# A planned instruction order is planned again: another cost table, a pause ahead of one kind of product, and a closing pair that takes its products in turn

## The chip, the cores and the metric

The kernel runs on one core of one Trainium2 chip. The metric is device time in microseconds (us) of the whole program; less is better. Times before the change are the median of three runs; the profile is of one more execution.

## The reference

Random-feature attention for 4 batches, 8 heads, 576 tokens, head size 64 and 128 features, then two layers of a two-matrix network over the 2304 tokens (width 512, inner width 2048):

```python
def phi(x):
    proj = np.einsum('bhsd,md->bhsm', x, omega)
    h = proj - np.sum(x * x, axis=-1, keepdims=True) / 2.0
    return np.exp(h - np.max(h, axis=-1, keepdims=True)) / np.sqrt(m)
q_p, k_p = (phi(q_s), phi(k_s))
kv = np.einsum('bhsm,bhsd->bhmd', k_p, v); z = np.sum(k_p, axis=2)
num = np.einsum('bhsm,bhmd->bhsd', q_p, kv)
den = np.einsum('bhsm,bhm->bhs', q_p, z)[..., None] + 1e-06
x = (num / den)            # to (2304, 512)
x = leaky_relu(x @ w1_in) @ w1_out
h = x @ w2_in
out = (h * np.clip(h + 3.0, 0.0, 6.0) / 6.0) @ w2_out
```

## The kernel before, in words

The tokens are cut into five row groups (GN: 512, 256, 512, 512, 512). Attention of a group makes its rows; **layer one** (moe1) runs group by group, with the attention of the next group put between its matmuls; **layer two** (moe2) follows in the order 0, 2, 3, 4, 1, so that the last row group is the one with 256 rows. Every large product is three matmuls (high by high, low by high, high by low part of fp32 numbers split in two).

In layer two a 512-row group takes its products by a scheme with seven products for a 2x2 block product. `Hpair` makes two blocks of the inner width: seven products of six matmuls each of 256 columns (line 1122), into three half banks R[0], R[1], R[2]. R[0] is used for four products in turn. Each is added onto the sum that the bank holds, and between them `save` copies R[0] out with ScalarE (`late_u<-bank`). So the second product into R[0] has to wait until the first one's copy is done, the third for the second one's, the fourth for the third one's. `parts` splits the result into two tiles of the kind g, with four additions of 128 columns (line 472 where GpSimd does them). `down` makes the seven products of the second matrix, three matmuls each (line 1044), and `finish` adds them up and stores them (lines 1065, 1069). The last row group has `Hsingle` (plain products, lines 478 to 480, 256 columns) instead of `Hpair`.

Nothing of the order is written by hand. Each step is an `op` with a due time, the engines that may do it and a cost on each; `Graph.run` keeps a clock for every engine and takes the step that can start first. All instructions are issued in that order, and each engine does its own in order. On TensorE, attention steps inside layer one are held back by SLACK, and by FOLLOW right behind another attention step, so that they come in groups; SWITCH is the planner's price for a change between attention and layers. `keep_warm` (line 1317) puts in matmuls on a zero tile where the planner sees TensorE idle before layer one begins: 15 at the start, and later one for every 326 ns of a gap. BIAS is what a step must save before it goes to VectorE; T0, L1, ATT, SG, UP, DOWN, XLEAD, SOON and READY are the due times; CAP and `room` set how many buffers a kind has.

## Time and profile before

| what | value |
|---|---|
| median of 3 runs | 907.85 us (905.75 to 908.74) |
| profiled execution, device time | 907.79 us |
| its span, first to last instruction | 906.0 us |
| TensorE busy | 892.0 us of the span |
| VectorE, ScalarE, GpSimd busy | 617.0, 492.8, 332.0 us |

The span is what the trace shows; 1.8 us of the device time lie around it. Matmuls are pipelined: one of 256 columns is shown some 280 ns long while the next one starts 113 to 118 ns after it. So a stretch is read by the starts of the instructions and by how many there are in it, not by the busy share, which is near 100% at any pace.

### The profile page before, as it was taken

The page shows a single profiled execution, that of the slowest core. Times are in us where ns is not written, and L with a number is a line of the kernel's source. Part 1 is how long each engine was busy: PE and PEld are TensorE (multiplying, and loading weights), DVE is VectorE, ACT ScalarE, POOL GpSimd, SP SyncE. Part 2 cuts the span into 40 slices and gives each one's busy share as a digit, 9 for nine tenths or more (in the row PEclk, how much of TensorE's full clock was granted, in tenths as well). Part 3 has the DMA queues.
Part 4 walks back from the last instruction along what each step waited for, and adds up shares of the span by engine and source line. Part 5 has one row for each costly group of instructions (what it writes and reads, how often), then busy time and mean ns, then how long its engine had stood idle before and what let it go on. Part 6 is the DMA issues. An engine that isn't in the chain of part 4 may idle for free.

```text
span 906.0 us, 17804 instructions
## 1 busy us (share of the span) xinstructions
PE 892.0 (98%) x6349; PEld 796.2 (88%) x6349; DVE 617.0 (68%) x1464; ACT 492.8 (54%) x1155; POOL 332.0 (37%) x559
## 2 busy tenths in 40 slices
PE   8999999999999999999999999999999999999998
PEld 8878888889777877888888888999999999999997
DVE  5998877877897976555687344675665658666554
ACT  6966674866776555544455345543443444445442
POOL 3454454544535321101010003244426436454642
PEclk9999999999999999999999999999999999999999
DMA  9556644677557555978899349885786684677540
GB/s 333 152 167 215 204 153 139 208 228 232 149 171 223 178 166 178 367 286 314 292 343 349 95 140 326 280 296 168 244 311 218 201 260 131 224 242 231 167 134 28
DMA packets 91497, 198.01 MB, mean 219 GB/s; under 512 B 14736, under 2 KB 40976, under 8 KB 91408
## 3 DMA queue, kind: packets, MB, share of 16 engines
q1 hardware_dynamic: 91408, 196.87, 65.7%
q8 instruction: 50, 0.82, 0.4%
q14 instruction: 39, 0.32, 0.1%
HBM read 150.18 MB, written 46.66 MB: 217 GB/s over the span
## 4 chain that ended last, share of the span: by engine, by line
PE 91%; DVE 4%; ACT 2%; issue 1%; DMA 1%; POOL 1%; SPq 0%; DVEq 0%; POOLq 0%; ACTq 0%
PE bank L1044 18%; PE bank L1122 17%; PE bank L478 15%; PE bank L480 15%; PE bank L479 15%; PE bank L721 4%; PE bank L768 1%; PE bank L949 1%; PE bank L918 1%; PE bank L790 1%; DVE junk L892 1%; PE bank L844 1%; DMA late_w<-in 1%; DVE nm L686 1%; PE bank L779 0%
## 5 line engine op out<-in xcount | busy, mean ns | idle before, releaser
L1044 PE MATMUL bank<-w,g 128*128 128x256 f32 x762 | 108.1, 279 | 0.4 <-DVE g L467 0.2
L1044 PEld LDWEIGHTS bank<-w,g 128*128 128x128 f32 x762 | 96.9, 188 | 1.0 <-DVE g L467 0.7
L464 ACT COPY late_u<-bank 128x256 f32<-128x256 f32 (+1 forms) x112 | 43.1, 386 | 95.1 <-PE bank L1122 86.4
L986 DVE TENSOR_TENSOR g<-bank,g 128x512 fp32r<-128x512 f32 (+1 forms) x80 | 50.8, 635 | 60.9 <-ACT g L464 60.2
L984 ACT ACTIVATE bank<-bank 128x512 f32<-128x512 f32 (+1 forms) x80 | 43.8, 548 | 76.2 <-PE bank L480 76.0
L1122 PE MATMUL bank<-x,late_w 128*128 128x256 f32 x552 | 74.0, 281 | 0.9 <-DVE u L1065 0.7
L697 ACT ACTIVATE h<-bank,nm 128x128 f32<-128x128 f32 x228 | 63.5, 390 | 18.9 <-POOL nm L692 18.7
L1122 PEld LDWEIGHTS bank<-x,late_w 128*128 128x128 f32 x552 | 68.2, 189 | 1.5 <-DVE u L1065 0.9
L1122 PE MATMUL bank<-second_w,late_w 128*128 128x256 f32 x498 | 68.5, 281 | 0.5 <-ACT late_u L464 0.5
L478 PE MATMUL bank<-g,w 128*128 128x512 f32 (+1 forms) x180 | 68.9, 383 | 0.0
L478 PE MATMUL bank<-x,w 128*128 128x512 f32 (+1 forms) x180 | 68.7, 382 | 0.1
L480 PE MATMUL bank<-g,w 128*128 128x512 f32 (+1 forms) x180 | 66.3, 368 | 0.8 <-DVE g L986 0.8
L480 PE MATMUL bank<-x,w 128*128 128x512 f32 (+1 forms) x180 | 66.4, 369 | 0.5 <-POOL x L468 0.5
L479 PE MATMUL bank<-g,w 128*128 128x512 f32 (+1 forms) x180 | 66.2, 368 | 0.0
L479 PE MATMUL bank<-x,w 128*128 128x512 f32 (+1 forms) x180 | 66.2, 368 | 0.0
L1122 PEld LDWEIGHTS bank<-second_w,late_w 128*128 128x128 f32 x498 | 62.4, 189 | 0.8 <-ACT late_u L464 0.7
L686 DVE TENSOR_REDUCE nm<-bank 128x4 f32<-128x512 f32 (+2 forms) x76 | 48.1, 654 | 15.8 <-PE bank L721 15.7
L1044 PE MATMUL bank<-second_w,g 128*128 128x256 f32 x333 | 48.8, 280 | 0.0
L903 POOL TENSOR_TENSOR h<-h,den 128x512 f32<-128x512 f32 (+2 forms) x32 | 33.1, 1038 | 41.8 <-DVE den L898 25.4
L692 POOL TENSOR_TENSOR nm<-nm,sq 128x4 f32<-128x4 f32 (+2 forms) x76 | 25.2, 344 | 60.2 <-DVE nm L689 57.2
L478 PE MATMUL bank<-x,second_w 128*128 128x512 f32 (+1 forms) x120 | 45.2, 377 | 0.3 <-ACT h L697 0.3
L472 POOL TENSOR_TENSOR xr<-late_xr 128x128 f32<-128x128 f32 x38 | 19.3, 526 | 70.7 <-DVE late_xr L1160 70.7
(361 smaller groups left out, 2449.9 us busy)
## 6 DMA issues: line engine op xcount, KB each, us to landing
late_w<-in SPq DMA_DIRECT2D x84, 512.0 KB, 4.5
in<-late_w SPq DMA_DIRECT2D x32, 512.0 KB, 3.8
late_w<-in SPq DMA_DIRECT2D x40, 256.0 KB, 4.5
third_w<-in SPq DMA_DIRECT2D x20, 512.0 KB, 4.4
wst<-w2i SPq DMA_DIRECT2D x16, 512.0 KB, 4.2
wst<-w2o SPq DMA_DIRECT2D x16, 512.0 KB, 4.1
x_t<-late_w SPq DMA_DIRECT2D x12, 512.0 KB, 4.5
wst<-w1i SPq DMA_DIRECT2D x10, 512.0 KB, 4.6
```

The source lines that it names most:

```text
L464: return [("act", c_act(n, psum), lambda: nc.scalar.copy(dst(), src())), dve if psum else dve + (True,)]
L478: nc.tensor.matmul(o, lhsT=ah, rhs=bh, start=start, stop=False)
L479: nc.tensor.matmul(o, lhsT=al, rhs=bh, start=False, stop=False)
L480: nc.tensor.matmul(o, lhsT=ah, rhs=bl, start=False, stop=stop)
L686: g.op([("dve", c_dve(c * 128), lambda raw=raw, n_=n_: nc.vector.tensor_reduce(out=n_()[:, :, 0], in_=raw(), axis=AX.X, op=ALU.min))], rd= ...
L697: nc.scalar.activation(h.tiles[0][:, q * 128:q * 128 + 128], raw()[:, q], AF.Exp, bias=nm.tiles[0][:, q], scale=-1.0)
L721: nc.tensor.matmul(ps[bank].tiles[0][o, at:at + 128], lhsT=src.tiles[0][r, k * one + i * 128:k * one + i * 128 + n], rhs=wn[r], start=True ...
L903: eng.tensor_tensor(out=x, in0=x, in1=den.tiles[1][:, 0:c].to_broadcast([128, c, 128]), op=ALU.mult)
L984: g.op([("act", c_act(n, True), lambda: nc.scalar.activation(P(), P(), AF.Prelu, alpha=0.01))], wr=[p], due=d)
L986: g.op([("dve", c_dve(n), lambda: nc.vector.tensor_tensor(out=G1(), in0=P(), in1=G0().bitcast(F32), op=ALU.subtract))], rd=[p, (gg, 0)], w ...
L1044: nc.tensor.matmul(acc[bank].tiles[0][:, half * 256:half * 256 + 256], lhsT=src.tiles[x][:, q * 128:q * 128 + 128], rhs=w[k].tiles[y][:, c ...
L1122: nc.tensor.matmul(R[r](), lhsT=w[x], rhs=m[y], start=start and k == n == 0, stop=k == 1 and n == 2, skip_group_check=True)
```

## The change

The planner gets another table of numbers and four new rules. (1) TensorE steps of attention have a mode: S (scores, 64-row tiles), N (the products with 64-column tiles) or F (the others); a table TURN gives the price of each change of mode, and WAIT, MATE and FOLLOW say how long a step waits for company. (2) `Hpair` gives every later product into R[0] a lag of APART, 100 ns of the planner's time, so that other work goes between. (3) In the last row group the last two pairs take products 4 to 7 in turn, with due times 100 ns apart, in the order b11, t2, t3, b21, t1, t4, b22. (4) `finish` of that group has a tile more for its sums and another order of additions. Besides, the transposed inputs of the first stage have four buffers for three, LAT is 165 for 150, BIAS2 200 for 300, and due times and buffer counts differ. The arithmetic is the same.

```diff
-SLACK = 2000.0
-FOLLOW, SWITCH = 400.0, 110.0
+SLACK = 1.0
+PACE = 2.215
+WAIT = {"S": 4000.0, "N": 1000.0, "F": 1500.0}
+FOLLOW = 400.0
+MATE = 400.0
+TURN = {("M", "S"): 193.0, ("M", "N"): 92.0, ("S", "M"): 205.0, ("N", "M"): 158.0, ("F", "S"): 193.0, ("F", "N"): 97.0, ("S", "F"): 175.0,
...
-NW1 = 10
+NW1 = 11
-BIAS2 = 300.0
+BIAS2 = 200.0
-UP, DOWN = 7.2e3, 2.5e3
+UP, DOWN = 7100.0, 2600.0
+APART = 100.0
-LAG_A, XLEAD, SOON, READY = 3.0, 9e3, 10e3, 14e3
+LAG_A, XLEAD, SOON, READY = 2.5, 6000.0, 13000.0, 15000.0
...
-    LAT = 150.0
+    LAT = 165.0
-    CAP = {"x2": 5, "s": 2, "h": 4, "sum": 4, "raw": 6}
+    CAP = {"x2": 6, "s": 1, "h": 6, "sum": 4, "raw": 6}
...
-                at = o.ready + (FOLLOW if o.slack and last else o.slack) + o.lazy
+                at = o.ready + (self.wait(o.mode, last) if o.slack else 0.0) + o.lazy
...
-                if last != (o.slack > 0.0):
-                    clock["pe"] += SWITCH
-                    o.end += SWITCH
-                last = o.slack > 0.0
+                turn_ = TURN.get((last, o.mode), 0.0)
+                clock["pe"] += turn_
+                o.end += turn_
+                last = o.mode
...
+    def wait(mode, last):
+        if mode == "F":
+            return FOLLOW if last != "M" else WAIT["F"]
+        return MATE if last in "SN" else FOLLOW if last == "F" else WAIT[mode]
...
-    first, more = room("first", [("h", 6, ([128, 512], F32)), ("xT", 3, ([128, 512], F32)), ("xn", 2, ([128, 8, D], F32)),
+    first, more = room("first", [("h", 6, ([128, 512], F32)), ("xT", 4, ([128, 512], F32)), ("xn", 2, ([128, 8, D], F32)),
...
-    def down(acc, a, b, i, due, after=[]):
+    def down(acc, a, b, i, due, after=[], close=None):
...
-        for k in (0, 1, 4, 5, 3, 2, 6) if i == FT // 2 - 1 else range(7):
+        order = [0, 4, 5, 1, 3, 2, 6] if close is not None else [0, 1, 4, 5, 3, 2, 6] if i == FT // 2 - 1 else range(7)
+        for at, k in enumerate(order):
             src, q, x = todo[k]
+            if close is not None and at > 2:
+                due = close + 100.0 * (2 * at + (i == FT // 2 - 1))
...
+        if rows[0] == GT[ORDER2[-1]]:
+            o.append(Buf("u", line="o"))
+            add(2, 0, (0, 1), P6)
+            add(2, 1, (2, 0), P7)
+            add(0, 0, (0, 1), P2)
+            store(0, 0)
+            add(0, 1, (2, 0), P5)
+            add(1, 1, (2, 1), P5)
+            store(1, 1)
+            add(1, 0, (2, 1), P4)
+            store(1, 0)
+            add(0, 1, (0, 1), P3)
+            store(0, 1)
+            return
...
-                g.op([("pe", 6 * c_mm(256), mm)], rd=[c[a], b], wr=[bank[r]], due=t0 + UP * at)
+                g.op([("pe", 6 * c_mm(256), mm)], rd=[c[a], b], wr=[bank[r]], due=t0 + UP * at, lag=APART if r == 0 and not start else 0.0)
...
-                down(acc, a, b, k, T + (UP if fast else UP * 0.5) * (k + 1 + LAG_A))
+                last = grp == ORDER2[-1] and k >= NP - 2
+                down(acc, a, b, k, T + (UP if fast else UP * 0.5) * (k + 1 + LAG_A), [],
+                     T + UP * 0.5 * (NP + LAG_A) if last else None)
```

What this does to the order is shown at three places. In the changed kernel keep_warm is line 1349, the scores line 734, Hpair's products line 1152 and down's line 1057.

**The first stage**, TensorE, ahead of the first product of keys and values (L768, L781). `first_xT` are the transposed inputs of the scores. Before:

```order
L721 MATMUL bank_178<-wn,first_xT_2_0_166 128x128
L721 MATMUL bank_179<-wn,first_xT_2_0_166 128x128
L1317 MATMUL bank_182<-zero 128x384 x12
L768 MATMUL bank_180<-first_v_0_0_169,ht_0_152 128x132
L768 MATMUL bank_180<-first_v_0_0_169,first_h_0_0_158 128x66
```

With the change:

```order
L734 MATMUL bank_179<-wn,first_xT_2_0_166 128x128
L734 MATMUL bank_180<-wn,first_xT_2_0_166 128x128
L1349 MATMUL bank_183<-zero 128x384 x5
L734 MATMUL bank_181<-wn,first_xT_3_0_167 128x128
L734 MATMUL bank_182<-wn,first_xT_3_0_167 128x128
...
L1349 MATMUL bank_183<-zero 128x384 x4
L781 MATMUL bank_176<-first_v_0_0_170,ht_0_152 128x132
L781 MATMUL bank_176<-first_v_0_0_170,first_h_0_0_158 128x66
```

A fourth scores step (eight matmuls) stands ahead of the first product of keys and values. Over the whole stage 34 of the 45 zero matmuls are left; the other 204 matmuls are the same.

**Layer two**, TensorE, one pair of the first row group. Before, R[0] is bank2:

```order
L1122 MATMUL bank6_181<-second_w0_1_0_1021,late_w0_1_0_3976 128x256 x6
L1122 MATMUL bank2_177<-second_w0_4_0_1024,late_w0_1_0_3976 128x256 x6
L1044 MATMUL bank4_179<-w3_86,g1_106 128x256 x3
L1044 MATMUL bank5_180<-w12_95,late_g1_0_0_3979 128x256 x3
L1122 MATMUL bank2_177<-second_w0_3_0_1023,late_w0_0_0_3975 128x256 x6
L1044 MATMUL bank4_179<-w7_90,late_g1_0_0_3979 128x256 x3
L1044 MATMUL bank1_176<-w9_92,late_g1_0_0_3979 128x256 x3
L1122 MATMUL bank2_177<-x0_101,third_w2_0_0_1595 128x256 x6
```

With the change, R[0] is bank2 as well:

```order
L1152 MATMUL bank5_181<-w5_88,late_w0_2_0_3976 128x256 x6
L1057 MATMUL bank6_182<-w15_98,g1_106 128x256 x3
L1057 MATMUL bank4_180<-w15_98,g1_106 128x256 x3
L1152 MATMUL bank2_178<-w9_92,late_w0_2_0_3976 128x256 x6
L1057 MATMUL bank6_182<-second_w0_0_0_1054,g1_106 128x256 x3
L1057 MATMUL bank7_183<-w16_99,g1_106 128x256 x3
L1057 MATMUL bank4_180<-second_w0_4_0_1058,late_g1_0_0_3978 128x256 x3
L1152 MATMUL bank2_178<-second_w0_3_0_1057,late_w0_1_0_3975 128x256 x6
L1152 MATMUL bank3_179<-w0_83,late_w0_3_0_3977 128x256 x6
L1152 MATMUL bank1_177<-w1_84,late_w0_3_0_3977 128x256 x6
L1152 MATMUL bank2_178<-x0_101,third_w2_0_0_1613 128x256 x6
```

Between two products into the same R[0] stood six other matmuls, twice; now nine and twelve stand there. Over all of layer two, 96 products go into an R[0] that a copy has to clear first: before, 41 of them have six matmuls between, two have three and one has none; with the change five have six, one has none, and all others nine or more.

**The end**, TensorE, the last products. Before, in bank7, bank3, bank1 and bank0:

```order
L1044 MATMUL bank7_182<-second_w0_9_0_1029,g0_105 128x256 x3
L1044 MATMUL bank1_176<-third_w0_0_0_1593,g0_105 128x256 x3
L1044 MATMUL bank7_182<-w5_88,g2_107 128x256 x3
L1044 MATMUL bank3_178<-second_w0_2_0_1022,g2_107 128x256 x3
L1044 MATMUL bank3_178<-w5_88,g2_107 128x256 x3
L1044 MATMUL bank0_175<-second_w0_2_0_1022,g0_105 128x256 x3
L1044 MATMUL bank1_176<-third_w0_0_0_1593,g2_107 128x256 x3
```

With the change, in bank6, bank4, bank1 and bank5:

```order
L1057 MATMUL bank6_182<-second_w0_9_0_1063,g0_105 128x256 x3
L1057 MATMUL bank1_177<-second_w0_7_0_1061,g1_106 128x256 x3
L1057 MATMUL bank1_177<-third_w0_0_0_1611,g0_105 128x256 x3
L1057 MATMUL bank4_180<-second_w0_10_0_1064,late_g1_0_0_3978 128x256 x3
L1057 MATMUL bank5_181<-third_w1_0_0_1612,g1_106 128x256 x3
L1057 MATMUL bank6_182<-w0_83,g2_107 128x256 x3
L1057 MATMUL bank4_180<-w1_84,g2_107 128x256 x3
L1057 MATMUL bank4_180<-w0_83,g2_107 128x256 x3
L1057 MATMUL bank5_181<-w1_84,g0_105 128x256 x3
L1057 MATMUL bank1_177<-second_w0_7_0_1061,late_g1_0_0_3978 128x256 x3
L1057 MATMUL bank1_177<-third_w0_0_0_1611,g2_107 128x256 x3
```

Between the last pair's first product (g0 into bank6) and its second one into that bank stood three matmuls, now twelve. Behind the last product that VectorE needs twice (g2 into bank4) stood six matmuls at the end of the program, now twelve with the two of bank4.

## Rows read from the trace of the kernel before

**Rows 1.** The page: busy time, share and instructions of each engine.

```profile
PE 892.0 (98%) x6349; PEld 796.2 (88%) x6349; DVE 617.0 (68%) x1464; ACT 492.8 (54%) x1155; POOL 332.0 (37%) x559
```

**Rows 2.** Windows by stage: PE, PEld, DVE, ACT, POOL busy, clock, DMA.

```profile
0.00:49.30 49.30, 45.08 (x405) 41.09 (x405) 37.05 (x95) 39.51 (x113) 19.78 (x46) 1.00 0.73 248
...
536.00:901.70 365.70, 363.36 (x3073) 360.31 (x3071) 220.81 (x488) 165.43 (x338) 162.58 (x307) 1.00 0.67 219
```

**Rows 3.** Timeline of PE, first stage: start, us, line, tile, idle before.

```profile
1.12 4.45 PE L1317 MATMUL bank<-zero 128*128 128x384 f32 x15 [1.12 <-POOL zero L1308]
...
9.34 2.35 PE L1317 MATMUL bank<-zero 128*128 128x384 f32 x12
11.53 0.39 PE L768 MATMUL bank<-first_v,ht 128*128 128x132 f32 x2
...
37.82 1.48 PE L1317 MATMUL bank<-zero 128*128 128x384 f32 x7
40.48 0.65 PE L862 MATMUL bank<-ident,u 128*128 128x128 f32 x4 [1.18 <-DVE u L853]
```

**Rows 4.** Timeline of PE, one visit of attention inside layer one.

```profile
51.97 0.39 PE L480 MATMUL bank<-x,w 128*128 128x512 f32 x1
52.28 1.09 PE L742 MATMUL bank<-wn,xT 64*64 64x128 f32 x16
53.30 0.50 PE L478 MATMUL bank<-x,w 128*128 128x512 f32 x1
53.65 0.40 PE L479 MATMUL bank<-x,w 128*128 128x512 f32 x1
```

**Rows 5.** Windows of PE in layer two: us, busy (matmuls), clock, DMA.

```profile
592.00:620.00 28.00, 28.00 (x250) 1.00 0.76 265
824.00:852.00 28.00, 28.00 (x240) 1.00 0.56 174
...
880.00:899.00 19.00, 19.00 (x170) 1.00 0.18 62
...
560.00:869.00 309.00, 308.22 (x2634) 1.00 0.71 229
```

**Rows 6.** Timeline of PE, layer two, two places.

```profile
564.35 0.84 PE L1044 MATMUL bank<-w,g 128*128 128x256 f32 x6
565.02 0.92 PE L1122 MATMUL bank<-second_w,third_w 128*128 128x256 f32 x6
565.78 0.87 PE L1044 MATMUL bank<-w,g 128*128 128x256 f32 x6
...
591.60 0.88 PE L1122 MATMUL bank<-second_w,late_w 128*128 128x256 f32 x6
592.32 0.50 PE L1044 MATMUL bank<-second_w,late_g 128*128 128x256 f32 x3
592.66 0.84 PE L1044 MATMUL bank<-w,g 128*128 128x256 f32 x6
593.34 0.84 PE L1122 MATMUL bank<-x,late_w 128*128 128x256 f32 x6
```

**Rows 7.** ScalarE's copies out of R[0], 592 to 620 us: min/median/max ns.

```profile
L464 ACT COPY late_u<-bank x7: 373/373/374, 592.6 to 611.6; 128x256 f32<-128x256 f32 x7
```

**Rows 8.** Waits of PE in layer two: us in total, times, longest.

```profile
PE bank L1122 <- DVE u L1065: 0.7, 1, 0.7
```

**Rows 9.** Groups by form: an addition of 256 columns on VectorE.

```profile
L1065 DVE TENSOR_TENSOR late_u<-late_u,bank 128x256 f32<-128x256 f32 x49 | 19.4, 415 | 7.0 <-ACT late_u L464 3.7 <-PE bank L1044 2.8
```

**Rows 10.** Timeline, the end: all engines.

```profile
899.72 0.41 PEld L1044 LDWEIGHTS bank<-w,g 128*128 128x128 f32 x3 [0.32 <-ACT late_u L464]
...
901.07 1.87 DVE L1065 TENSOR_TENSOR late_u<-late_u,bank 128x256 f32<-128x256 f32 x5 [0.26 <-PE bank L1044]
...
901.20 0.50 PE L1044 MATMUL bank<-third_w,g 128*128 128x256 f32 x3
...
902.30 1.31 SPq L1069 DMA_DIRECT2D out<-late_u  x3
```

More of the change, by code (lines that the diff above doesn't have):

```diff
@@ L40 @@
 ORDERLY = ("first",)
-NW1 = 10
+NW1 = 11
 LEAD = 0.8
-BIAS2 = 300.0
+BIAS2 = 200.0
 PAD = 48
-O1, O2 = 11e3, 12e3
-T0 = 42e3
-L1 = [100e3, 50e3, 127e3, 87e3, 87e3]
-ATT = [None, (32e3, 132e3), (132e3, 182e3), (182e3, 240e3), (240e3, 300e3)]
-RAW = (150e3, 310e3)
-PREP = (330e3, 390e3)
+O1, O2 = 11000.0, 12000.0
+T0 = 42000.0
+L1 = [100000.0, 50000.0, 127000.0, 87e3, 87e3]
+ATT = [None, (32000.0, 132000.0), (132e3, 178000.0), (182e3, 236000.0), (240e3, 305000.0)]
+RAW = (150000.0, 302000.0)
+PREP = (330000.0, 400000.0)
 EARLYX = [0, 2, 3]
-UP, DOWN = 7.2e3, 2.5e3
-LAZY = 2e3
-LAG_A, XLEAD, SOON, READY = 3.0, 9e3, 10e3, 14e3
+UP, DOWN = 7100.0, 2600.0
+LAZY = 2000.0
+APART = 100.0
+LAG_A, XLEAD, SOON, READY = 2.5, 6000.0, 13000.0, 15000.0
 PARTS = [[(0, 4, False), (1, 0, True)], [(1, 1, True), (2, 3, False)], [(2, 1, False), (3, 3, True)], [(3, 0, True), (4, 4, False)]]
@@ L76 @@
 class Op:
-    __slots__ = ("alts", "due", "slack", "allocs", "bufs", "deps", "ndep", "out", "ready", "end", "eng", "seq", "phase", "second", "cost", "lazy")
+    __slots__ = ("alts", "due", "slack", "allocs", "bufs", "deps", "ndep", "out", "ready", "end", "eng", "seq", "phase", "second", "cost", "lazy", "mode")
 class Graph:
-    LAT = 150.0
+    LAT = 165.0
     MORE = {"dve": 80.0, "act": 90.0, "pool": 80.0}
@@ L100, in __init__, with op @@
         self.todo = {}
-    def op(self, alts, rd=(), wr=(), due=0.0, also=(), late=False):
+    def op(self, alts, rd=(), wr=(), due=0.0, also=(), late=False, lag=0.0, mode="F"):
         o = Op()
@@ L105, in op @@
         self.todo[o.phase] = self.todo.get(o.phase, 0) + 1
-        o.alts, o.due, o.seq, o.lazy = alts, due, len(self.ops), LAZY if late else 0.0
+        o.alts, o.due, o.seq, o.lazy = alts, due, len(self.ops), LAZY if late else lag
         o.slack = self.slack if alts[0][0] == "pe" else 0.0
+        o.mode = mode if o.slack else "M"
         o.out, o.ready, o.end, o.eng = [], 0.0, None, None
@@ L168, in run @@
         share = {"acc": 4, "H": H0, "att": 0, "first": 7}
-        last = False
+        last = "M"
         early = sum(any(b.use == "first" for b in o.allocs) for o in self.ops)
@@ L305, in before @@
     @staticmethod
+    def wait(mode, last):
+        if mode == "F":
+            return FOLLOW if last != "M" else WAIT["F"]
+        return MATE if last in "SN" else FOLLOW if last == "F" else WAIT[mode]
+    @staticmethod
     def before(start, o, best):
@@ L329, in c_mm @@
 def c_mm(n):
-    return 114.0 if n == 256 else max(112.0, n / 2.215)
+    return 114.0 if n == 256 else max(112.0, n / PACE)
 def c_dma(nbytes):
@@ L722, in mm @@
                                          rhs=wn[r], start=True, stop=True)
-        g.op([("pe", nh * (f + half) * 228.0, mm)], rd=[src], wr=ps, also=hs, due=due)
+        g.op([("pe", nh * (f + half) * 224.0, mm)], rd=[src], wr=ps, also=hs, due=due, mode="S")
         features(ps, hs, cols, before, sq, due, nh)
@@ L743, in mm @@
                                      start=True, stop=True)
-        g.op([("pe", HP * 228.0, mm)], rd=[src], wr=[p], also=[h], due=due)
+        g.op([("pe", HP * 224.0, mm)], rd=[src], wr=[p], also=[h], due=due, mode="S")
         features([p], [h], [HP], [0], sq, due)
@@ L791, in kvt @@
                                      start=i == 0, stop=i == 4)
-        g.op([("pe", 5 * 224.0, kvt)], rd=hs + [ht, v], wr=[p], also=[zr, kf], due=due + 3e3)
+        g.op([("pe", 5 * 224.0, kvt)], rd=hs + [ht, v], wr=[p], also=[zr, kf], due=due + 3e3, mode="N")
         mid = lambda: kf.tiles[0].rearrange("p h c -> p (h c)")[:, 0:128]
@@ L950, in num @@
                                      rhs=tq.tiles[0][:, e, k * n:k * n + n], start=True, stop=True)
-        g.op([("pe", max(230.0, N * 1.92), num)], rd=[tq] + kf, wr=[p], also=[x for x, _ in outs], due=due + 6e3)
+        g.op([("pe", max(214.0, N * 1.88), num)], rd=[tq] + kf, wr=[p], also=[x for x, _ in outs], due=due + 6e3, mode="N")
         for k, (hp, (xr, at)) in enumerate(zip(hps, outs)):
@@ L1243, in weights @@
                 Buf.NOW = 1 if i < NW1 else 2 if i < 2 * FT - 3 * ST2 // 2 else 0
-                d.append(weight(src, j, SG[0] + step * (j + o) - 4e3))
+                d.append(weight(src, j, SG[0] + step * (j + o) - 4000.0))
         Buf.NOW = 0
```

1 line of the change is left out of this document (added).

## The prediction

> **What bounds the kernel now.** I read the page first: TensorE is busy for 892.0 us of the 906.0 us span, 98%; no other engine is over 68% [rows 1]. So the time is the time of TensorE's instructions one behind another, and the question is what it spends beside its work. Then the windows by stage [rows 2]. The first stage, to 49.3 us, has TensorE 45.1 us busy, but part of that are matmuls on a zero tile [rows 3]. Layer two, 536 to 901.7 us, has 363.4 of 365.7 us busy. The reader is to see that in these two stages busy is not the same as useful.
>
> For layer two the windows of TensorE alone show it [rows 5]. In the 28 us from 592 it runs 250 matmuls, in the 28 us from 824 it runs 240, all of 256 columns. Two or three at the edges are counted in part, so that is 0.113 us each in the one and 0.118 in the other. The timeline shows what changes the pace [rows 6]: six matmuls of down start at 564.35 and the next at 565.02, 0.68 us for six, the quick pace. Then a product of Hpair into R[0], with six matmuls between it and its forerunner, takes 0.76 us, and the next matmuls go at the slow pace. At 591.60 such a product came in the slow pace; it took 0.72 us (0.71 is the slow pace), and by 592.66 six take 0.68 again. So that kind of product costs 0.03 us in the slow pace and 0.055 in the quick one, and it turns the one pace into the other. The reason is in the copy: ScalarE needs 0.373 us for it [rows 7], a matmul is shown 0.28 us long, and with some 0.05 us for the two signals that makes 0.70 us from the last matmul's start to a free R[0]. Six matmuls between are seven starts, 7 x 0.113 = 0.79 us, but the weights of the waiting product are loaded one matmul ahead, at 0.68 us. It is just too late, nearly every time.
>
> From 560 to 869 us there are 2634 matmuls in 309 us [rows 5]. At the quick pace they would take 2632 x 0.1133 = 298.2 us, so 10.8 us are lost. Some 38 late products at 0.037 (27 of 41 at 0.03, 14 at 0.055) are 1.4 us; two long waits, one of them on VectorE [rows 8], some 1.3 us. About 8.0 us are left for the slow pace: at 0.0044 us more each, some 1800 matmuls, two thirds of the stretch.
>
> **The change part by part**, against the profiled execution's own 907.79 us (its span of 906.0 and 1.8 around it; the median of the runs, 907.85, is the same within 0.1).
>
> First stage, -2.8 us. 11 of the zero matmuls go. The twelve stand from 9.34 to 11.53 us, 2.19 us; seven stand from 37.82 and with the wait behind them last to 40.48, 2.66 us [rows 3]. Together 4.85 us for 19, 0.255 each: 11 x 0.255 = 2.8. They go because work moves into the gap: a fourth scores step stands ahead of the first product of keys and values. Bounds: nothing, if that gap and the later ones are set by ScalarE and VectorE, which have 39.5 and 37.1 us of work in these 49.3 [rows 2]; and 11 x 0.38 = 4.2, if all are as dear as the seven. ScalarE has three copies of 512 columns and two conversions fewer ahead of the first layer matmul, so there is room. I take the middle.
>
> Attention inside layer one, +0.2 us. A visit of scores costs beside its own work 0.31 - 0.23 us on the way in and 0.35 - 0.23 on the way out [rows 4], 0.2 us. Counted in the order, there are 72 visits of attention for 71 before: the new prices move the visits, they don't join more of them. Two visits fewer or four more bound it, -0.4 and +0.8. The Trainium skill (TensorEngine Tiling (Array Packing), Key Properties) says that changing the tiling mode drains TensorE; by that rule alone this part would be the gain, but the count shows nothing to gain, and the row agrees with the rule on the price.
>
> Late products in layer two, -1.3 us: 41 with six matmuls between become five, 36 x 0.037. Bounds 36 x 0.03 and 36 x 0.055, so 1.1 and 2.0. With nine between there are 0.34 us more, and no such product is late.
>
> The pace of layer two, -4.5 us. With the change four of the late products and the one with nothing between stand in the first 165 matmuls of layer two, and the next stands 2166 matmuls in, 918 ahead of the end. A long wait, as the one with nothing between makes, mostly leaves the quick pace; the late product at 2166 leaves the slow one. Before, the last row group had the quick pace again by 880 us (170 matmuls in 19 us, [rows 5]), some 190 to 270 matmuls ahead of the end. That makes about 100 + 650 slow matmuls, say 800, for 1800: 1000 x 0.0044 = 4.4, with the few slow ones outside the stretch 4.5. Bounds: -8.0, if it is quick throughout, and +5, if it falls into the slow pace early and nothing takes it out.
>
> The end, -0.8 us. At 899.72 TensorE lost 0.32 us to ScalarE's copy of the last pair's first product, since only three matmuls stood between [rows 10]; twelve cover it. TensorE is done at 901.70; VectorE's five additions last to 902.94, and the three last stores go out one behind another from 902.30 to 903.61, 0.44 each. With the change the additions of the second use of bank4 are done some 0.4 us before the end; of the last two the one starts with TensorE's end, the other 0.33 later, done at 902.5, and the last store goes out at 902.6 for 903.2, 0.55 less. Bounds 0 and -1.1.
>
> Nothing: 170 of the 288 additions of 128 columns in layer two go from GpSimd to VectorE. At most 0.415 us each, the row of 256 columns [rows 9], they add 71 us to 220.8 busy of 365.7 [rows 2]: at most 80%. What hides them is the time between a pair's last product and its use; if that cover is gone, they are the rival below. Later due times, buffer counts and one weight more in the first stage move work that is off TensorE's path.
>
> Sum: -2.8 + 0.2 - 1.3 - 4.5 - 0.8 = -9.2: **898.6 us**.
>
> **The rivals.** *The slow pace stays.* For it: 27 of the 41 late products, met in the slow pace, left it slow more often than not, and one wait of 0.7 us [rows 8] left it slow too; with fewer disturbances there are fewer ways out. Against it: the quick pace has only been lost to late products. It takes back the 4.5: 903.1; at the worst, slow from end to end, 908. *The first stage is set by the other engines.* For it: ScalarE is busy for four fifths of it, VectorE for three quarters [rows 2], each in its own order. Against it: TensorE's longest wait there is 1.18 us [rows 3]. The 2.8 are gone: 901.4. *Quick throughout*: 8.0 for 4.5 and 4.2 for 2.8, 893.7.
>
> *VectorE comes late (slower).* In its order four additions of a pair now stand between others that TensorE waits for. 170 are some 42 sets of four. If TensorE waits 0.42 us at each, as long as one addition, that is 17.6 us: 916. It decides from 9.2 / 42 = 0.22 us a set for no gain, and 0.28 for slower. For it: TensorE has waited 0.7 us for VectorE once [rows 8]. Against it: on GpSimd the same four took longer, and between the last write of a tile and its first use stand at least eleven matmuls with the change, nine before.
>
> *The clock.* The granted clock is 1.00 in both stages, the 2.4 GHz level [rows 2], and the longest idle time in the first one is 1.18 us [rows 3]. If without the 11 it fell to 1.2 GHz, the stage's zero matmuls give the price: 0.30 us each in the first 4.45 us against 0.18 later [rows 3]; ten us of work so slowed would cost some 6 us and eat two thirds of the gain: 904.8. The Trainium skill (TensorE: Matmul & The Clock Gate, HAM oscillation) warns of idle gaps between bursts, which speaks against taking such matmuls away; no row of this case shows a fall. *No effect*: the due times bring as many new long waits as old ones go, 3 to 5 us more, and the first stage gives nothing: 906.
>
> **How the numbers follow.** 0.3%, 2.7 us, is about what a measurement of this kernel tells from no change. Forecast 0.55; slow pace stays 0.15; first stage bound elsewhere 0.10; quick throughout 0.07; no effect 0.06; VectorE late 0.05; clock 0.02. Faster: the first four and the clock, 0.89, less 0.02 for the worst of the slow pace: 0.87. Same 0.07, slower 0.06. The range reaches to quick throughout below (893.5) and past the slow pace above (904.5); beyond it lie no effect, VectorE late and the ends of the others.
>
> **What would show it.** The first layer matmul at 46.5 us for 49.3; some 245 to 250 matmuls in most windows of 28 us in layer two, 240 only near its start and in the last row group; products into R[0] at 0.68 us; no idle time of TensorE on ScalarE near the end, and 4.3 us from its last matmul to the end made 3.7. The forecast is wrong if layer two runs 240 per 28 us through whole row groups, if the first layer matmul stays at 49, or if TensorE's waits for VectorE in layer two come to several us.

## The result, and the profile after

The change is faster: 897.4 us, median of six runs (895.36 to 901.0), for 907.27 before; ratio 0.9902, 95% interval 0.9878 to 0.9926. Four later executions (run 5 below) gave 0.9875 (0.9862 to 0.9888). The prediction was 898.6, from 893.5 to 904.5. The profiled execution is the slowest of the six, with 901.0 us and a span of 898.9, so its rows show 6.8 of the 9.9 us.

The page's busy row, and the windows by stage, with their bounds moved to the changed kernel's own stages (us, then PE, PEld, DVE, ACT, POOL busy, granted clock, DMA share and GB/s):

```profile
PE 886.6 (99%) x6338; PEld 792.3 (88%) x6338; DVE 660.4 (73%) x1663; ACT 480.1 (53%) x1127; POOL 243.3 (27%) x388
```

```profile
0.00:46.35 46.35, 42.84 (x394) 39.40 (x394) 36.18 (x96) 36.74 (x108) 16.02 (x44) 1.00 0.75 253
536.00:895.05 359.05, 355.29 (x3038) 352.31 (x3036) 258.06 (x671) 160.30 (x324) 70.05 (x132) 1.00 0.66 218
```

Against [rows 1, 2]: TensorE's 892.0 is 886.6, eleven matmuls fewer; VectorE took over additions that GpSimd gave up, and is busy for 72% of layer two. The first stage is 3.0 us shorter. The timeline of TensorE at its end:

```profile
42.69 1.29 PE L1349 MATMUL bank<-zero 128*128 128x384 f32 x6
44.75 0.66 PE L875 MATMUL bank<-ident,u 128*128 128x128 f32 x4 [0.77 <-DVE u L866]
45.33 1.09 PE L734 MATMUL bank<-wn,xT 64*64 64x128 f32 x16
46.35 0.50 PE L491 MATMUL bank<-x,w 128*128 128x512 f32 x1
```

The first layer matmul starts at 46.35, for 49.3 [rows 2], behind a wait for VectorE that no zero matmul fills. In the other executions of the changed order it starts between 45.55 and 46.40.

The pace in layer two, windows of TensorE (us, busy and matmuls, clock, DMA), first the changed kernel:

```profile
592.00:620.00 28.00, 28.00 (x240) 1.00 0.61 218
660.00:688.00 28.00, 28.00 (x249) 1.00 0.82 293
740.00:768.00 28.00, 28.00 (x250) 1.00 0.42 137
824.00:852.00 28.00, 28.00 (x240) 1.00 0.45 142
560.00:869.00 309.00, 306.79 (x2642) 1.00 0.68 226
```

Compare [rows 5]: 250 matmuls in 28 us is the quick pace, 240 the slow one, and the change from 2634 to 2642 in the long window is small. By the starts of the matmuls, the pace changed 21 times between 549 us and the end before, and most stretches lasted under 20 us. Now whole row groups go at one pace: from 552 to 628 us it is slow, to 784 quick, to 863 slow, and quick from there. Counted by the starts of the 256-column matmuls, 1357 of some 3000 are 116 to 119 ns behind their forerunner, 1853 before. Where the count begins and how strictly the bounds are taken moves such a count by up to 20.

The waits of TensorE in layer two (what for, us in total, times, longest) against [rows 8]:

```profile
PE bank L1152 <- DMA late_w<-in: 1.4, 2, 1.2
PE bank L1057 <- ACT bank L1185: 0.9, 1, 0.9
PE bank L1152 <- DMA third_w<-in: 0.5, 1, 0.5
PE bank L1152 <- ACT u L477: 0.5, 1, 0.5
PE bank L1057 <- DVE g L480: 0.2, 1, 0.2
```

One, for a DMA that loads weights, cost 1.2 us and ended at 717.8 us. The 0.7 us for VectorE's u is gone.

The end, timeline of all engines, against [rows 10]:

```profile
892.74 1.44 PEld L1057 LDWEIGHTS bank<-w,g 128*128 128x128 f32 x12
...
894.55 0.50 PE L1057 MATMUL bank<-third_w,g 128*128 128x256 f32 x3
...
895.09 0.42 DVE L1081 TENSOR_TENSOR late_u<-late_u,bank 128x256 f32<-128x256 f32 x1
...
895.42 0.41 DVE L1081 TENSOR_TENSOR u<-late_u,bank 128x256 f32<-128x256 f32 x1
...
896.08 0.40 SPq L1085 DMA_DIRECT2D out<-u  x1
```

The twelve weight loads have no idle time ahead of them, where 0.32 us stood. TensorE ends at 895.05 and the span at 898.9: 3.8 us for 4.3.

### The profile page after: what moved, and what is told of

The parts are those of the page before. It is cut to its first block, busy times and chain, and to the rows that moved or that the text cites. A ratio compares the mean times of both kernels' runs of the same rounds, so it can differ in the third digit from the quotient of the medians.

```text
span 898.9 us, 17816 instructions
## 1 busy us (share of the span) xinstructions
PE 886.6 (99%) x6338; PEld 792.3 (88%) x6338; DVE 660.4 (73%) x1663; ACT 480.1 (53%) x1127; POOL 243.3 (27%) x388
## 4 chain that ended last, share of the span: by engine, by line
PE 91%; DVE 4%; DMA 3%; ACT 1%; POOL 1%; issue 0%; SPq 0%; DVEq 0%; POOLq 0%
PE bank L1057 19%; PE bank L1152 16%; PE bank L491 15%; PE bank L493 14%; PE bank L492 14%; PE bank L734 4%; PE bank L781 2%; PE bank L962 1%; DMA late_w<-in 1%; PE bank L803 1%; PE bank L931 1%; DVE junk L905 1%; DMA third_w<-in 1%; PE bank L857 1%; DMA first_xT<-qT 1%; DVE nm L699 1%
## 5 line engine op out<-in xcount | busy, mean ns | idle before, releaser
L477 ACT COPY late_u<-bank 128x256 f32<-128x256 f32 (+1 forms) x98 | 37.8, 385 | 112.5 <-PE bank L1152 95.4
L1057 PE MATMUL bank<-w,g 128*128 128x256 f32 x633 | 88.2, 279 | 1.3 <-ACT bank L1185 0.9
L1057 PEld LDWEIGHTS bank<-w,g 128*128 128x128 f32 x633 | 79.6, 188 | 2.1 <-ACT bank L1185 1.1
L1152 PEld LDWEIGHTS bank<-x,late_w 128*128 128x128 f32 x576 | 70.0, 188 | 1.7 <-DVE u L1163 1.4
L699 DVE TENSOR_REDUCE nm<-bank 128x4 f32<-128x512 f32 (+2 forms) x76 | 47.1, 655 | 16.3 <-PE bank L734 14.6
L1057 PE MATMUL bank<-second_w,g 128*128 128x256 f32 x387 | 55.6, 278 | 0.0
L1152 PE MATMUL bank<-w,late_w 128*128 128x256 f32 x384 | 52.6, 279 | 0.2 <-DMA late_w<-in 0.2
L1057 PEld LDWEIGHTS bank<-second_w,g 128*128 128x128 f32 x387 | 49.6, 188 | 0.0
L1152 PEld LDWEIGHTS bank<-w,late_w 128*128 128x128 f32 x384 | 48.3, 189 | 0.6 <-DMA late_w<-in 0.4
L905 DVE CUSTOM_DVE_ANT_0 junk<-h,zr 128x128 bf16<-128x128 f32 (+1 forms) x128 | 46.0, 397 | 1.3 <-ACT zr L477 0.3
```

Source lines behind the costliest of these rows:

```text
L477: return [("act", c_act(n, psum), lambda: nc.scalar.copy(dst(), src())), dve if psum else dve + (True,)]
L699: g.op([("dve", c_dve(c * 128), lambda raw=raw, n_=n_: nc.vector.tensor_reduce(out=n_()[:, :, 0], in_=raw(), axis=AX.X, op=ALU.min))], rd= ...
L905: nc.vector.tensor_tensor_reduce(out=jk.tiles[0][r, q % 2], in0=h.tiles[0][r, q * 128:q * 128 + 128], in1=zr[k].tiles[0][r, e], scale=1.0, ...
L1057: nc.tensor.matmul(acc[bank].tiles[0][:, half * 256:half * 256 + 256], lhsT=src.tiles[x][:, q * 128:q * 128 + 128], rhs=w[k].tiles[y][:, c ...
L1152: nc.tensor.matmul(R[r](), lhsT=w[x], rhs=m[y], start=start and k == n == 0, stop=k == 1 and n == 2, skip_group_check=True)
```

## The experiments

All ratios are to the kernel before, run beside each on the same chip, with 95% intervals. "Slow" counts layer two's matmuls that start 116 to 119 ns behind their forerunner, in the one profiled execution. Late products are starts 20 to 100 ns later than the pace has them; waits of over 100 ns are read from the starts in the same way.

### 1. The pause alone

```diff
+APART = 100.0
...
-        o.alts, o.due, o.seq, o.lazy = alts, due, len(self.ops), LAZY if late else 0.0
+        o.alts, o.due, o.seq, o.lazy = alts, due, len(self.ops), LAZY if late else lag
...
-                g.op([("pe", 6 * c_mm(256), mm)], rd=[c[a], b], wr=[bank[r]], due=t0 + UP * at)
+                g.op([("pe", 6 * c_mm(256), mm)], rd=[c[a], b], wr=[bank[r]], due=t0 + UP * at, lag=APART if r == 0 and not start else 0.0)
```

> The kernel before with the pause ahead of later products into R[0] and nothing else of the change: of 96 such products two have six matmuls between and three have none, where 41, two with three, and one stood. The first stage and the end are those of before. Theory (a late product costs 0.037 us and sets the slow pace, and without it the quick pace lasts): 1.3 us for the late products and 2 to 4.5 us for the pace, less up to 1 us for the two more that wait with nothing between, so 902 to 905 us, ratio 0.994 to 0.997, and fewer than 1000 of layer two's matmuls at 0.118 us. Rival one (the pace has another cause): 905.5 to 906.5, about 1800 matmuls at 0.118 as before. Rival two (the products that are moved up bring new waits): 907 or more.

Measured: 906.54 us, ratio 0.9995 (0.9983 to 1.0006). Late products of 20 to 100 ns cost 0.3 us for 1.7, as forecast, but waits of over 100 ns rose from 4.5 to 6.2 us, and 1720 matmuls were slow. So rival one had the pace, and the time but for 0.04 us; of rival two the new waits are there, 1.7 us, and not its time of 907 or more. The windows of TensorE:

```profile
592.00:620.00 28.00, 28.00 (x240) 1.00 0.76 266
660.00:688.00 28.00, 28.00 (x240) 1.00 0.88 316
...
824.00:852.00 28.00, 28.00 (x249) 1.00 0.63 200
```

And the place where the quick pace was lost, PE and PEld on the timeline:

```profile
586.14 0.84 PE L1123 MATMUL bank<-second_w,late_w 128*128 128x256 f32 x6
586.95 0.77 PEld L1123 LDWEIGHTS bank<-w,late_w 128*128 128x128 f32 x6 [0.17 <-DVE g L468]
586.98 0.94 PE L1123 MATMUL bank<-w,late_w 128*128 128x256 f32 x6
...
587.76 0.52 PE L1123 MATMUL bank<-second_w,late_w 128*128 128x256 f32 x3
```

A weight load came 0.17 us late, and from there 1123 matmuls ran slow, to 720 us. This is no later product into R[0] with six between. The prediction's sentence that the quick pace is only lost to those is wrong.

### 2. The buffer caps alone

```diff
-    CAP = {"x2": 5, "s": 2, "h": 4, "sum": 4, "raw": 6}
+    CAP = {"x2": 6, "s": 1, "h": 6, "sum": 4, "raw": 6}
```

> The kernel before with the changed buffer caps alone (h 6 for 4, s 1 for 2, x2 6 for 5). That alone brings the zero matmuls of the first stage from 45 to 34, and leaves layer two's late products (42 with six between) and its end as they were. Theory (the first stage is worth 0.255 us for each zero matmul): first layer matmul at 46.4 us for 49.3, and 904 to 905 us, ratio 0.996 to 0.997. Rival (what the first stage gives is lost again in the layers): first layer matmul at 46.4 and 906.5 to 908.

Measured: 906.2 us, ratio 0.9988 (0.9973 to 1.0002). The first layer matmul came at 47.11 us, 2.2 earlier, and layer two gave most of it back: 1917 slow, 0.36 us more behind the last matmul, and 2.3 us more in late starts, 8.5 for 6.2. Of these 2.3 some 1.4 are a fall of the granted clock, on the timeline and in the window of TensorE:

```profile
556.64 1.58 PE L1122 MATMUL bank<-w,late_w 128*128 128x256 f32 x6 [1.04 <-DVE late_u L1133]
```

```profile
558.00:560.00 2.00, 2.00 (x12) 0.50 1.02 372
```

TensorE waited 0.86 us at 553.8 and 1.04 us at 555.6. From 556.7 to 560.1 us the granted clock was 0.50, the 1.2 GHz level, and fourteen matmuls started 213 to 218 ns apart. Late products alone cost 1.5 us for 1.7, as before. Six of the twelve executions show a mean clock of 0.997 or 0.998 as this one does, of the kernel before none. The caps shorten the first stage, but they also hold for layer two; the rival is nearer.

### 3. The change without the pause

```diff
-APART = 100.0
+APART = 0.0
```

> The changed kernel with the pause at zero: 20 later products into R[0] have six matmuls between and five have three, where five have six now; first stage and end are those of the change. Theory: late products and short waits 20 x 0.037 and 5 x 0.35, some 2.5 us, and the slow pace for more of layer two, 0 to 3 us more, so 899.5 to 903 us, ratio 0.991 to 0.995 against before (0.990 for the change). Rival (the new due times make the gain, not the pause): 897 to 898.5.

Measured: 904.0 us, ratio 0.9963 (0.9948 to 0.9977), against 0.9875 and 0.9902 for the change: the pause, with the other order that the planner makes for it, is worth 5.5 to 8 us there, more than expected. In the profile 2429 matmuls are slow; against the changed kernel's first profile the slow pace costs 4.8 us more and late products 1.4, while long waits cost 0.7 less. All windows read are slow:

```profile
592.00:620.00 28.00, 28.00 (x240) 1.00 0.60 212
...
740.00:768.00 28.00, 28.00 (x241) 1.00 0.42 141
824.00:852.00 28.00, 28.00 (x238) 1.00 0.41 130
```

### 4. The old close

```diff
-                     T + UP * 0.5 * (NP + LAG_A) if last else None)
+                     None)
```

and `finish` without its new branch.

> The changed kernel with the old order of the last row group's last products and of its additions. Theory: TensorE waits 0.3 us again for the last pair's copy, and from its last matmul to the end it is 4.3 us again, so 0.7 us more than the change: 898.1 us, ratio 0.991. Rival (the last stores set the end either way): as the change, 897.4, and 3.85 us after the last matmul.

Measured: 899.91 us, ratio 0.9916 (0.989 to 0.9942); the interval holds both expectations. The rows show the mechanism. On the timeline of the end the copy's wait is back, and the last five additions run as one row:

```profile
894.70 1.45 PEld L1057 LDWEIGHTS bank<-w,g 128*128 128x128 f32 x12 [0.31 <-ACT late_u L477]
...
896.04 1.87 DVE L1081 TENSOR_TENSOR late_u<-late_u,bank 128x256 f32<-128x256 f32 x5 [0.26 <-PE bank L1057]
```

4.29 us lie behind the last matmul. So by the rows the close is worth 0.31 and some 0.45, 0.75 us; the times do not decide it.

### 5. The change again

No edit.

> The changed kernel as it is, profiled and timed once more. Theory now (the pace is a state that a late product or a wait of a weight load ends, and that a later wait gives back or doesn't, differently from one execution to the next): its runs spread over 4 to 6 us, and this profile's own time differs from 901.0 by about 0.0045 us for each matmul of layer two that it has more or fewer than 1357 at 0.118 us, within 1 us. Rival (the spread of the runs lies elsewhere, in DMA or in the first stage): time and number of slow matmuls don't go together.

Measured: 896.47 us, median of four (895.38 to 896.61), ratio 0.9875 (0.9862 to 0.9888). The profiled execution took 896.61 us, with 774 slow matmuls for 1357: 2.6 us less by the theory, of 4.4. The other 1.8 are 1.25 of long waits and 0.6 of the first stage, so the expectation of 1 us was missed; the pace is the largest part all the same. The four runs spread over 1.2 us, not 4 to 6. The windows:

```profile
592.00:620.00 28.00, 28.00 (x240) 1.00 0.61 221
660.00:688.00 28.00, 28.00 (x250) 1.00 0.82 288
...
824.00:852.00 28.00, 28.00 (x250) 1.00 0.50 150
560.00:869.00 309.00, 307.74 (x2675) 1.00 0.68 227
```

The window from 824 was slow in the first profile and is quick in this one: the same instructions in the same order.

### 6. The pause and the caps

The edits of 1 and 2 together in the kernel before.

> The kernel before with the pause and the buffer caps, and nothing else of the change: 34 zero matmuls in the first stage, two products into R[0] with six matmuls between and three with none. Theory (the parts add up): -0.5 of the pause alone and -1.1 of the caps alone, and 0.9 for the late products that the caps alone had more, so 904.5 to 905.5 us, ratio 0.997. Rival one (the two together let the quick pace last, as in the change): 900 to 902, ratio 0.992 to 0.994, under 1000 slow matmuls. Rival two (the due times and the grouping of the change carry the rest): no more than 905.5 either, and what is missing to 897.4 is in long waits and visits.

Measured: 903.68 us, ratio 0.9952 (0.9939 to 0.9966), between the theory and rival one; 1740 slow, first layer matmul at 47.11, waits of over 100 ns 6.9 us. The 0.9 us for late products in my expectation came from run 2's profile, where it was the fall of the clock; two of the six executions here show a mean clock of 0.998, the profiled one 1.00. The pause and the caps make 3.8 of the 9.9 us, and more than the sum of each alone. The rest was not tried rule by rule: the due times, LAT and the fourth buffer were changed in no run by themselves. Between this profile and those of the change the rest lies in slow matmuls (1740 for 1357 and 774), visits (95.5 us for 94.0), the first stage (47.1 for 46.35 and 45.75) and the end.

### 7. A probe for the pace

```diff
             def prod(r, a, off, b, at, start):
                 def mm():
+                    if r == 0 and start and (i % 2 == 0):
+                        nc.tensor.matmul(p.tiles[0][:, 0:64], lhsT=c[a].tiles[0][0:64, off:off + 128], rhs=b.tiles[0][0:64, 0:64],
+                                         start=True, stop=True, skip_group_check=True)
+                    if r == 0 and start and (i % 2 == 1):
+                        nc.tensor.matmul(p.tiles[0][:, 0:64], lhsT=c[a].tiles[0][:, off:off + 128], rhs=b.tiles[0][:, 0:64],
+                                         start=True, stop=True, skip_group_check=True)
```

> The changed kernel with 32 short matmuls more in layer two, one ahead of the first product of each pair into R[0], which writes over it: for even pairs on 64 rows (another tile mode), for odd pairs on 128 rows, both with 64 columns. It measures what takes the slow pace away. Theory: the 64-row one empties TensorE's pipeline as a change of mode does in layer one and leaves the quick pace in over 12 of 16, for 0.25 to 0.45 us each; the 128-row one costs 0.05 to 0.12 and leaves the pace as a late product of that size does, mostly slow. Sum 32 us x 0.1 to 0.4 / 1, so 3 to 8 us for the inserted work less up to 5 for the pace: 897 to 904 us. Rival (the pace is set by something outside TensorE's order, memory traffic say): the pace after either form is as before it, and 901 to 906 us.

Measured: 910.37 us, ratio 1.0033 (1.0022 to 1.0043), outside both expectations: I had taken half of layer two as won for the quick pace, but each 128-row matmul loses what the 64-row one has given, and 2165 matmuls were slow. As a probe it shows that TensorE's own order changes the pace, and the rival of a cause outside it fell. Of the sixteen on 64 rows, fourteen came in the slow pace, and behind all fourteen it was the quick one. Of the sixteen on 128 rows, fourteen came in the quick pace, and behind all fourteen it was the slow one. But the two kinds stand in turn, so nearly each met the pace that the other had left. Of those that did not, the 64-row one at 546.6 us came in the quick pace and left the slow one, and of two 128-row ones that came in the slow pace the one at 539.1 left the quick pace and the one at 794.0 the slow one. The sixteenth on 64 rows stands behind matmuls of 512 columns. So it is not shown that each form has a pace of its own; that a short matmul mostly turns the pace into the other one fits this run as well. Four 64-row ones that came in the quick pace and left it quick, in runs 8 and 11, and one on 128 rows that came slow and left slow, in run 12, speak for the former. The timeline of TensorE at one of each kind:

```profile
613.54 0.84 PE L1158 MATMUL bank<-x,late_w 128*128 128x256 f32 x6
614.22 0.19 PE L1152 MATMUL bank<-x,late_w 128*128 128x64 f32 x1
614.25 0.95 PE L1158 MATMUL bank<-x,late_w 128*128 128x256 f32 x6
615.04 0.52 PE L1057 MATMUL bank<-second_w,g 128*128 128x256 f32 x3
615.39 0.52 PE L1057 MATMUL bank<-w,g 128*128 128x256 f32 x3
615.75 1.58 PE L1057 MATMUL bank<-second_w,g 128*128 128x256 f32 x12
```

```profile
625.99 0.87 PE L1158 MATMUL bank<-x,late_w 128*128 128x256 f32 x6
626.79 0.29 PE L1149 MATMUL bank<-x,late_w 64*128 64x64 f32 x1
627.01 1.64 PE L1158 MATMUL bank<-x,late_w 128*128 128x256 f32 x12
628.50 0.50 PE L1057 MATMUL bank<-second_w,g 128*128 128x256 f32 x3
628.84 0.39 PE L1057 MATMUL bank<-third_w,g 128*128 128x256 f32 x2
```

In the first, six take 0.68 us ahead of the short matmul and the three from 615.39 take 0.36, 0.118 each. In the second, the three from 628.50 take 0.34, 0.113 each. The 128-row one costs 0.115 us by the starts (28 and 200 ns, for one of 113), the 64-row one 0.42 (209, 223 and 222 ns, for two of 117). The Trainium skill (TensorEngine Tiling (Array Packing), Key Properties) says that a change of the tiling mode drains TensorE; the starts agree, since the waits stand on both sides of the short matmul.

### 8. Three resets, and where they stood

The edit goes into the changed kernel's `Hpair`, where the probe stood.

```diff
+RESET = ((0, 1), (3, 2), (4, 2))
...
+                    if r == 0 and start and (grp, i) in RESET:
+                        nc.tensor.matmul(p.tiles[0][:, 0:16], lhsT=c[a].tiles[0][0:64, off:off + 128], rhs=b.tiles[0][0:64, 0:16],
+                                         start=True, stop=True, skip_group_check=True)
```

> The changed kernel with three short matmuls on 64 rows more (16 columns, written over by the product behind them), one ahead of a pair each: in the first row group's second pair and in the third and fourth row group's third pair, behind places where the pace was lost in the profiles of the change. Theory (such a matmul costs 0.42 us and brings the quick pace back each time): 1.3 us for the three, less 2.5 us at the first place in every execution, some 2 at the third and 0.8 at the second on the mean, so 893 to 894.5 us, ratio 0.984 to 0.986, with fewer than 500 slow matmuls in the profile and a smaller spread than the change's 895.4 to 901.0. Rival (the pace falls back by itself, and the resets only cost): 898 to 899.

Measured: 898.58 us (893.5 to 901.55), ratio 0.9913 (0.9889 to 0.9936): as the rival has it. But I had misread the places: a pair's first product is issued earlier than its number says, and the three came at 538, 699 and 775 us. The first turned the slow pace into the quick one; the other two stood in the quick pace already, and it was lost behind them, at 549.8, 780 and 862 us, 1132 slow in all. The run says little more than what three resets cost.

### 9. The old grouping of attention

```diff
-        if mode == "F":
-            return FOLLOW if last != "M" else WAIT["F"]
-        return MATE if last in "SN" else FOLLOW if last == "F" else WAIT[mode]
+        return FOLLOW if last != "M" else 2000.0
...
-                turn_ = TURN.get((last, o.mode), 0.0)
+                turn_ = 110.0 if (last == "M") != (o.mode == "M") else 0.0
```

> The changed kernel with the old rule for attention in layer one (one wait of 2000 and one price of 110 for any change, no modes); layer two's order stays that of the change, and there are 73 visits for 72. Theory (the count of visits sets the cost): 0.2 to 0.3 us more than the change, 896.5 to 898. Rival (the new rule puts visits where nothing waits in them, 1.7 us in the profile): 898 to 899.5, and the visits sum to 95.5 us or more for 94.0.

Measured: 895.99 us, ratio 0.9892 (0.9873 to 0.991), as the change. The visits sum to 94.7 us for 94.0 and layer one is no longer for it. The modes and their prices, the change's longest rule, do nothing that can be measured. The profiled execution took 893.34 us with 103 slow matmuls, the fewest seen:

```profile
592.00:620.00 28.00, 28.00 (x250) 1.00 0.61 211
...
560.00:869.00 309.00, 307.71 (x2700) 1.00 0.69 229
```

The first of these windows is quick here and slow in both profiles of the change, at the same DMA share of 0.61.

### 10. The additions back on GpSimd

```diff
-BIAS2 = 200.0
+BIAS2 = 300.0
```

> The changed kernel with the old price for VectorE in layer two, so that additions go back to GpSimd. Theory (they lie beside TensorE's work): 896.5 to 898.5, as the change. Rival one (VectorE's load sets buffers and waits): 894 to 896. Rival two (GpSimd is too late for TensorE): 899 to 903, with waits of TensorE for GpSimd in the trace.

Measured: 899.74 us, ratio 0.9934 (0.9912 to 0.9956), so 3 to 5 us more than the change by the medians of the ratios, though the interval touches that of the first runs. In the profiled execution, 899.24 us, it is not the pace: some 630 matmuls are slow, fewer than either profile of the change. It is rival two in size, and not in its place. TensorE's waits in layer two:

```profile
PE bank L1152 <- DMA late_w<-in: 1.4, 3, 0.6
PE bank L1057 <- DVE g L480: 1.1, 3, 0.4
...
PE bank L1057 <- DVE u L1081: 0.3, 1, 0.3
```

None is for GpSimd. TensorE waits for VectorE's g, which is made behind those additions: my reading is that they come late on GpSimd and g with them, but no run separates this from the other order that the planner made with the number. Waits of over 100 ns sum to 8.1 us for 5.0 to 6.3, and 0.6 us more lie behind the last matmul.

### 11 and 12. Two resets at the right places, and two on 128 rows

Against run 8, and run 12 against run 11:

```diff
-RESET = ((0, 1), (3, 2), (4, 2))
+RESET = ((0, 4), (4, 4))
```

```diff
-                        nc.tensor.matmul(p.tiles[0][:, 0:16], lhsT=c[a].tiles[0][0:64, off:off + 128], rhs=b.tiles[0][0:64, 0:16],
+                        nc.tensor.matmul(p.tiles[0][:, 0:16], lhsT=c[a].tiles[0][:, off:off + 128], rhs=b.tiles[0][:, 0:16],
```

> The changed kernel with two short matmuls on 64 rows (16 columns), at layer two's matmuls 249 and 2230, behind the two places where the profiles of the changed order lost the pace (near 553 and 785 us). The three of the run before stood at 66, 1444 and 2105, ahead of those places. Theory: 0.31 us each; from 563 us on the pace is quick in every execution, as from 794 on, so under 400 slow matmuls in the profile and 893 to 895.5 us, ratio 0.9845 to 0.988. Rival (the pace goes its own way): 896.5 to 898.

> The same two short matmuls at the same places, of the same 16 columns, but on all 128 rows, so without a change of the tile mode. Theory: 0.1 us each, less than the two on 64 rows, but both leave the slow pace, which then lasts to the next long wait (some 540 and 510 matmuls): 898 to 900 us, ratio 0.990 to 0.993, so 3 us and more above the run with 64 rows. Rival (a short matmul does nothing to the pace): 0.4 us under the run with 64 rows.

Measured: 896.94 us, ratio 0.9903 (0.9884 to 0.9922), with 64 rows; 898.13, ratio 0.9921 (0.9896 to 0.9946), with 128. The order of the two is that of the theory, the difference is 1.2 us for 3, and the intervals overlap: not decided by the times. The profiles have 463 and 1285 slow matmuls. With 64 rows the pace is quick behind both places, but it had come quick to both in this profile, and it was lost again 18 us behind the first one, where a weight load of a product came 0.13 us late at 580.9, and 383 ran slow to 627. With 128 rows the first one stood in the slow pace, which went on to 627; behind the second one, with a late weight load beside it, it was quick, against the theory; and 513 matmuls ran slow from 645, where neither stands. A quick pace holds only to the next disturbance, and such a matmul costs 0.4 us, not the 0.31 that I gave it. No version here is faster than the change beyond its interval.

## Why the prediction was right, and where not

**The time** was right, 897.4 for 898.6, and so was the list of places but for the visits, the long waits and the additions. The parts in both profiles of the changed kernel (901.00 and 896.61 us), against the profiled execution before:

| term | forecast | first profile | second |
|---|---|---|---|
| first stage | -2.8 | -3.0 | -3.6 |
| visits of attention | +0.2 | -1.7 | -1.8 |
| late products, 20 to 100 ns | -1.3 | -1.3 | -1.2 |
| slow pace | -4.5 | -2.2 | -4.8 |
| waits over 100 ns in layer two, without the copy at the end | 0 | +2.0 | +0.8 |
| the end, with that copy | -0.8 | -0.8 | -0.8 |

The columns sum to -7.0 and -11.4, for -6.8 and -11.2 measured. That the sum came out is in part luck: the visits gave 2 us more than forecast, and long waits that stood in the sum at nothing took 0.8 to 2.0 back.

**First stage**: right, somewhat low. I had put it to the zero matmuls that go; that number came down by the caps alone (run 2), not by the fourth buffer of transposed inputs that I described beside it. There the eleven brought 2.2 us, 0.20 each for my 0.255; what brings the other 0.7 to 1.5 us of the changed order was not tried. The rival that ScalarE and VectorE set the stage fell, though its end is now a wait for VectorE. The granted clock stayed at 1.00, the 2.4 GHz level, with eleven fewer, so the clock rival fell for the changed kernel. What the Trainium skill warns of (TensorE: Matmul & The Clock Gate, HAM oscillation) did not come true in its rows; run 2's rows show such a fall, in layer two and behind two waits.

**Visits**: wrong, by 2 us. I counted them and priced the way in and out, and did not look at the waits inside: one visit before had TensorE waiting 1.1 us for GpSimd's h from 238 us on, and that wait is gone:

```profile
239.22 0.55 PE L918 MATMUL bank<-ident,h 128*128 128x128 f32 x3 [1.14 <-POOL h L903]
```

In run 9's profile the old grouping rule costs 0.7 of it in the visits' sum, and nothing in the time; what brought the rest was not tried by itself.

**Late products**: right. Starts that come 20 to 100 ns late are 5 in layer two for 43, and 4 to 11 in the other runs with the pause; they cost 0.04 to 0.08 us each. Three of the five are the second start behind a longer wait. My sum for the lateness was short: at 564 us the copy starts 0.036 us behind the end of the bank's last matmul and the weight load 0.051 behind the end of the copy, 0.087 for the 0.05 that I gave both; with that the 0.055 us come out.

**Pace**: the mechanism was right only in part, and the size comes out at -2.2 and -4.8 us for -4.5, in the slowest of six executions and in one below the median. By its own sign (240 in 28 us through whole row groups) the first profile speaks against the forecast in two row groups. I had counted 100 slow matmuls at the start of layer two and 650 near its end. The first profile has some 630 from 552 to 628 us and 660 from 784 to 863, the second 615 and 63. In the first profile the quick pace was lost behind these two, the one a long wait and the other a product of `down` whose second matmul starts 194 ns behind its first; neither is a late product into R[0]:

```profile
551.78 0.95 PE L1057 MATMUL bank<-w,g 128*128 128x256 f32 x6 [0.93 <-ACT bank L1185]
...
784.18 0.59 PE L1057 MATMUL bank<-third_w,g 128*128 128x256 f32 x3
```

That late products switch the pace is shown: in the thirteen profiles without the probe, behind 41 of 45 single late starts of 45 to 110 ns in the quick pace it was the slow one. That nothing else does was wrong. Of the waits behind which the next matmul starts 0.19 us later, as where a weight load waits (run 1), 6 of 15 turned the quick pace into the slow one. Behind those of 0.1 us and more after which it starts 0.22 us later the pace is mostly quick, for 34 of 42 that came in the quick pace and 31 of 41 that came in the slow one; behind the rest it is slow. So with 36 of the 41 late products away the pace depends on a dozen other places and on chance. That is the reasoning of the rival that the slow pace stays, fewer disturbances are fewer ways out, and run 1 is that rival in full: the pause alone left 1720 slow. In the changed order the number of slow matmuls went from 103 to 2168 with layer two's order the same but for the close or two or three short matmuls (runs 4, 5, 8, 9, 11, 12 and the first profile), and the time with it, from 893.3 to 903.1 us. Each profile's time less 0.0045 us a slow matmul and less 0.42 or 0.115 an inserted one is 891.6 to 893.4, but for the first, 894.9, with its 1.2 us wait for a DMA. So across these seven profiles the pace explains nearly all of the spread.

**Nothing for the additions**: wrong by the run that puts them back (3 to 5 us), by whatever path; no row of the changed kernel says how much of its gain this is.

**VectorE late** fell: its waits sum to 0.2 us in layer two. **The end**: right.

## What to carry to other kernels

A stream of equal matmuls ran at two paces here, and the window counts show which; look for it before costing single waits. A start that came 0.08 us late cost some 2.9 us behind it (first profile, 784 us: 660 matmuls at 0.0044), so a change in the order is worth what it does to the pace, and that is known only on the mean of several executions. Where a table of numbers replans the whole program, change one number at a time: the longest rule of this change did nothing that could be measured, and its parts do not add up.

## What the runs showed of the hardware

- 256-column matmuls ran at 113.3 or 117.7 ns from start to start at a granted clock of 1.00, with the same instructions and the same order. The slow pace lasted for up to 1242 (run 4, 716 to 863 us), the quick one for 2870 (run 9, 554 to 887 us), each through a few late starts and waits. The Trainium skill (TensorE: Matmul & The Clock Gate, Back-to-back issue gap) has the spacing in a stream set by the weight load and the matmul together, without a value for 256 columns, and for an isolated matmul 262 cycles, by estimate 109 ns at 2.4 GHz; the rows show two spacings, both longer.
- A short matmul on 128 rows turned the quick pace into the slow one in 14 of 14, at 0.115 us, and one on 64 rows the slow pace into the quick one in 14 of 14, at 0.42 us; the few that met the other pace went both ways (runs 7, 8, 11 and 12). Why the pace changes there is not shown.
- Behind two waits of 0.86 and 1.04 us the granted clock fell to 0.50 for 3.4 us (run 2, 556.7 us), which cost some 1.4 us; single waits of up to 1.2 us in the profiles of the change left it at 1.00.
- What the two paces are inside TensorE stays open. The weight loads start 110 ns ahead of their matmul in the one and 114 in the other, and that is all that the records tell.
